# Sparse attention with a Swish layer: pair 1's first keys by the hardware queues, as f32

## Chip, cores and metric

One core of one Trainium2 chip. The kernel is launched once, and the metric is the device time of that launch in microseconds. Shorter is better.

## What is computed

Four batches of eight heads, 768 positions, 64 values per head, all inputs f32. Each position attends to its near neighbours (distance under 16) and to 24 block keys (the elementwise maximum over 32 keys) whose values are block means. The result goes through a two-matrix layer with a Swish of its own factor per channel.

```python
k_sum = k.reshape(B, H, nb, block, D).max(axis=3)        # block = 32, nb = 24
v_sum = v.reshape(B, H, nb, block, D).mean(axis=3)
scores_l = scale * q @ k.T ; mask_l = abs(i - j) < 16
scores_s = scale * q @ k_sum.T + log(block)
a = softmax([where(mask_l, scores_l, -1e9), scores_s])
x = a @ [v, v_sum]                                       # -> [3072, 512]
h = x @ w_in                                             # d_ff = 2048
out = (h / (1 + exp(-beta * h))) @ w_out
```

## The kernel before

The matrix products run on TensorE in bf16. Heads go in pairs, two heads of 64 on the 128 partitions; pair 0 is heads 0 and 1. The order of the work on each engine is the order in which the code is written: no scheduler moves it.

Batch 0 is done in two halves of 384 positions, so that the first half can enter the layer early. The part of the code that the change touches is the start of that first half. For each pair, `turn0(g)` turns the keys and queries with TensorE transposes (`pk`, `pq` in PSUM) and copies them to `kw` and `qt`. `scores0(g)` adds the mask and the scores into PSUM and takes the exponential on ScalarE. `max_k` makes the block keys on VectorE, `sum_v` the block means of v on TensorE (`vm_ps`). `pq` and `vm_ps` take turns in two PSUM buffers of the tag "t": what takes a buffer waits for the copy that empties it. `keep_warm(n)` issues n matmuls whose result nobody reads.

The code between two calls sets the order: `keep_warm`, `turn0(0)`, `turn0(1)`, `keep_warm(2)`, `scores0(0)`, `scores0(1)`, `turn0(2)`, `turn0(3)`, `scores_blk(0)`, `sum_v(0)`, `scores0(2)`, `scores0(3)`, `sum_v(1)` and so on, later `sum_v(3)` and the first products with `w_in`. The copies of the keys of pairs 0, 1 and 3 are ScalarE's, the copies of the queries of pairs 0, 1 and 2 and of the keys of pair 2 are VectorE's.

Loads are issued by three engines, each with its own queue. SP and ScalarE have hardware queues, whose transfers keep the type: pair 0's keys come as f32 into `k_f32` by SP and pair 0's queries into `q_f32` by ScalarE. VectorE casts the keys to bf16, ScalarE the queries. All other loads of batch 0 are issued by GpSimd, whose queue casts f32 to bf16 on the way (`load_k`, `load_q`, `load_v`), in the order of the code: keys of pair 1, queries of pair 1, keys of pairs 2 and 3, queries of pairs 2 and 3, v, `w_in`.

The cast also lays pair 0's keys out anew: in bf16 they stand as (j h d) instead of (h j d), so that one 128x128 transpose turns two heads at once. `turn` knows this as `packed`, six transposes a pair instead of twelve. The profile shows the tile `k_f32` as `k_f`, and `q_f32` as `q_f`.

Of the kernel before, what the change touches and what calls it, by code (L numbers as in the profile page):

```python
# [12 lines left out]
def kernel(  # L13
# [10 lines left out]
    nc = tc.nc  # L24
    ctx.enter_context(tc.manual_schedule(engines={getattr(mybir.EngineType, e) for e in ("SP", "Pool", "PE", "DVE", "Activation")}))
    P = 128
    f32 = mybir.dt.float32
# [4 lines left out]
    B, H, S, D = q.shape  # L32
    block = 32
    W = 16
# [6 lines left out]
    J = S // P  # L41
# [21 lines left out]
    const = ctx.enter_context(tc.tile_pool(name="consts", bufs=1))  # L63
# [9 lines left out]
    k_run = k.rearrange("b h (p j) d -> b p h (j d)", j=J)  # L73
    q_run = q[0].rearrange("h (u p j) d -> u p h (j d)", p=QP, j=JQ)
# [8 lines left out]
    kw_bufs = [const.tile([P, 2, NC, P], bf16, name=f"kw{i}") for i in range(NKW)]  # L83
    qt_bufs = [const.tile([P, nch, 2, QT], bf16, name=f"qt{i}") for i in range(NKW)]
    qk_bufs = {nm: const.tile([P, H, J * D], bf16, name=nm + "_all") for nm in "kq"}
    k_f32 = const.tile([P, 2, J * D], f32, name="k_f32")
    q_f32 = const.tile([QP, 2, JQ * D], f32, name="q_f32")
    q0_bufs = [const.tile([QP, H, JQ * D], bf16, name=f"q0_{i}") for i in range(2)]

    nat = {}  # L90
    dve, act, pool = nc.vector.tensor_copy, nc.scalar.copy, nc.gpsimd.tensor_copy
# [3 lines left out]
    def load_k(b, g, n=1):  # L95
        t = qk_bufs["k"][:, 2 * g:2 * (g + n)]
        nc.gpsimd.dma_start(out=t, in_=k_run[b, :, 2 * g:2 * (g + n)])
        for i in range(n):
            nat[("k", b, g + i)] = t[:, 2 * i:2 * i + 2]

    def load_q(u, g, n=1):
        t = q0_bufs[u][:, 2 * g:2 * (g + n)]
        nc.gpsimd.dma_start(out=t, in_=q_run[u, :, 2 * g:2 * (g + n)])
        for i in range(n):
            nat[("q", "q2")[u], 0, g + i] = t[:, 2 * i:2 * i + 2]
# [17 lines left out]

    beta_tmp = wpool.tile([k2, P], f32, name="beta_tmp")
    v_tail = wpool.tile([W, D], f32, name="v_tail")
    nc.sync.dma_start(out=k_f32[:], in_=k_run[0, :, 0:2])
    nc.scalar.dma_start(out=q_f32[:], in_=q_run[0, :, 0:2])
    nc.sync.dma_start(out=v_tail[:], in_=v_rows[0, H * S - W:H * S])
    nc.sync.dma_start(out=beta_tmp[:], in_=moe_beta.rearrange("(a p) -> a p", p=P))

# [20 lines left out]
    def fill(t, x):  # L151
        nc.vector.memset(t, x)

    def select(t, base, pattern, cm, op=ALU.is_ge, value=0.0):
        nc.gpsimd.affine_select(out=t, in_=t, compare_op=op, fill=value, base=base, pattern=pattern, channel_multiplier=cm)
# [2 lines left out]
    zero(identity)  # L158
    fill(near2, 1.0)
    fill(near, 1.0)  # L160
    load_k(0, 1)
    select(identity, 0, [[-1, P]], 1, ALU.not_equal, 1.0)
    load_q(0, 1)
    load_k(0, 2, 2)
    load_q(0, 2, 2)
    select(near2, -1, [[1, P + 32]], -1)
# [94 lines left out]
    def kw_of(b, g):  # L261
        return kw_bufs[(b * npair + g) % NKW]

    def flat_k(b, g):
        return kw_of(b, g)[:, 0].rearrange("p c f -> p (c f)")

    def flat_q(g):
        return qt_bufs[g].rearrange("p m r f -> p (m r f)")
# [18 lines left out]
    def psum(shape, dt, name, tag):  # L287
        if tag == "t":
            return ps.tile(shape, dt, name=name, tag="t", bufs=2)
        flat = take(name, dt)[:, 0, 0:math.prod(shape[1:])]  # L290
        if len(shape) == 2:
            return flat
        return flat.rearrange("p (a b) -> p a b", b=shape[2])

    def turn(nm, b, g, dst, copy, tag="t", packed=False):
        t = nat.pop((nm, b, g))
        n, js = t.shape[0], t.shape[2] // D
        p = psum([P, js, n], bf16, "p" + nm, tag)
        for j in range(js):
            if packed:  # L300
                nc.tensor.transpose(p[:, j], t.rearrange("p h f -> p (h f)")[:, j * P:(j + 1) * P], identity[0:n, 0:n])
                continue
            for h in range(2):
                nc.tensor.transpose(p[h * D:(h + 1) * D, j], t[:, h, j * D:(j + 1) * D], identity[0:n, 0:n])
        copy(out=dst.rearrange("p (t j) -> p t j", j=js), in_=p.rearrange("p j t -> p t j"))  # L305
# [98 lines left out]
    kq_of = {}  # L404

    def turn0(g, copy_k=act, copy_q=dve):
        turn("k", 0, g, flat_k(0, g)[:, W:W + S], copy_k, "big", g == 0)
        turn("q", 0, g, flat_q(g)[:, 0:HQ], copy_q, "t", g == 0)

    def scores0(g):  # L410
# [292 lines left out]
        for _ in range(n):  # L703
            nc.tensor.matmul(w_ps[:, 0:w], warm[:, 0:P], warm[:, 0:w], start=True, stop=True)

    for nm, t, copy, src in (("k", qk_bufs["k"][:, 0:2], dve, k_f32), ("q", q0_bufs[0][:, 0:2], act, q_f32)):
        nat[(nm, 0, 0)] = t
        copy(out=t.rearrange("p h f -> p (h f)").rearrange("p (j h d) -> p h j d", h=2, d=D),
             in_=src.rearrange("p h (j d) -> p h j d", d=D))
    keep_warm(9)  # L710
# [3 lines left out]
    fill(neg_m[0:W, 0:P], NEG)  # L714
    keep_warm(2)
    turn0(0)
    turn0(1)
    keep_warm(2)
    max_k(0, 0)
    scores0(0)  # L720
    max_k(0, 1)
    scores0(1)
    act(out=ve_bufs[0][0:W, HC, 0:D], in_=v_tail[:])
    turn0(2, dve, dve)
    turn0(3, act, act)
    scores_blk(0)
# [100 lines left out]
    for b in range(B):  # L827
# [6 lines left out]
        main, t = [], 0.0  # L834
# [33 lines left out]
        if b == 0:  # L868
# [23 lines left out]
            for g in pairs:  # L892
                t = dn0 + OT * TK[g] if g < 2 else up1 + TK[g]
# [15 lines left out]
        elif nxt < B:  # L909
            for g in pairs:  # L910
                t = (2.6, 6.5, 10.4, 14.3)[g]
# [60 lines left out]
```

## Time and profile before

| | |
|---|---|
| median of 3 runs | 213.62 us (213.19 to 213.9) |
| the profiled execution | 212.49 us |
| its span, from the first to the last instruction | 210.8 us |
| TensorE, matmuls | 201.4 us busy, 96% |
| VectorE | 109.4 us, 52% |
| ScalarE | 118.4 us, 56% |
| GpSimd | 80.9 us, 38% |
| granted TensorE clock | 1.000 |

Busy time counts an engine's instructions, without register, branch, semaphore and DMA-issuing ones on most engines. In the profile PE is TensorE's matmul, PEld its weight load, DVE VectorE, ACT ScalarE, POOL GpSimd and SP the engine that only issues transfers; a trailing q (ACTq) is the engine's issuing side. A row of the timeline gives start, duration, engine, line, operation, output<-input, shapes, the count merged into it (x6), and in brackets the idle time before it with what ended it. A row of the chain gives start, duration and what the end waited for.

### The profile page before, as it was taken

The numbers are of one execution on the slowest core, as the hardware profiler recorded it, in microseconds if no ns is written. First come the engines' busy times: TensorE is split into PE (matmuls) and PEld (weight loads), VectorE is DVE, ScalarE is ACT, GpSimd is POOL, SyncE is SP. The second block draws the span as 40 slices with busy tenths as digits, with TensorE's granted clock in tenths as the row PEclk, the third lists the DMA queues.
The fourth block names the chain that finished last, engine by engine and source line by source line (L and its number), as shares of the span: only waits on it lengthen the run. The fifth ranks groups of instructions, "written<-read, shape, count | busy, mean of one in ns | idle before, by whom it ended". The sixth has DMA issues, their size and how long they took to land.

```text
span 210.8 us, 4942 instructions
## 1 busy us (share of the span) xinstructions
PE 201.4 (96%) x2025; PEld 112.9 (54%) x2044; DVE 109.4 (52%) x311; ACT 118.4 (56%) x170; POOL 80.9 (38%) x116
## 2 busy tenths in 40 slices
PE   7798999999999999999999999999999999999993
PEld 2466654556545556565555456655555566654452
DVE  4877999997959869234726755514425000002120
ACT  3673988159797386668337256669165176640000
POOL 7995997495055399886300093000000000000000
PEclk9999999999999999999999999999999999999999
DMA  6999999999959999999994799900342500001212
GB/s 156 172 150 203 203 183 195 200 153 209 163 89 147 115 198 138 149 164 157 154 202 128 128 153 154 182 13 0 120 107 72 155 2 3 0 0 51 103 50 100
DMA packets 92055, 26.46 MB, mean 126 GB/s; under 512 B 81136, under 2 KB 89088, under 8 KB 92032
## 3 DMA queue, kind: packets, MB, share of 16 engines
q0 software_dynamic: 63888, 13.34, 77.5%
q1 hardware_dynamic: 27792, 12.40, 31.0%
q10 hardware_dynamic: 352, 0.39, 0.6%
q8 instruction: 16, 0.26, 0.5%
q14 instruction: 7, 0.06, 0.1%
HBM read 27.27 MB, written 6.29 MB: 159 GB/s over the span
## 4 chain that ended last, share of the span: by engine, by line
PE 90%; DMA 5%; issue 1%; DVE 1%; ACT 0%
PE h_ps L609 36%; PE o_ps L660 34%; PE o_ps L691 5%; PE h_ps L639 4%; DMA ve<-in_v_dram 3%; PE av_ps L566 3%; DMA k_f<-in_k_dram 2%; PE s_ps L521 2%; PE s_ps L504 1%; PE vm_ps L370 1%; PE px L487 1%; PE vm_ps L380 1%; PE av_ps L450 0%; PE s_ps L416 0%; DVE qt L305 0%
## 5 line engine op out<-in xcount | busy, mean ns | idle before, releaser
L609 PE MATMUL h_ps<-xT,w_in_sb 128*128 128x384 bf16 x464 | 76.7, 326 | 0.0
L660 PE MATMUL o_ps<-w_out_sb,h_sb 128*128 128x512 bf16 (+2 forms) x336 | 72.9, 369 | 1.8 <-issue 1.4
L621 ACT ACTIVATE h_sb<-h_ps,beta_sb 128x768 bf16<-128x768 f32 (+1 forms) x80 | 59.2, 773 | 23.3 <-PE h_ps L609 19.4
L609 PEld LDWEIGHTS <-w_in_sb 128*128 128x128 bf16 x464 | 45.0, 98 | 29.7
L660 PEld LDWEIGHTS <-h_sb 128*128 128x128 bf16 x352 | 32.6, 98 | 35.6
L679 DVE COPY o_sb<-o_ps 128x512 f32<-128x512 f32 x5 | 3.5, 691 | 38.6 <-PE o_ps L660 38.6
L547 DVE TENSOR_TENSOR attn<-attn,band 128x768 bf16<-128x768 bf16 x24 | 13.0, 556 | 19.0 <-ACT attn L496 17.3
L110 POOL DMA_DIRECT2D q_all<-in_q_dram x24 | 20.2, 869 | 3.5 <-DMA ve<-in_v_dram 3.1
L679 ACT COPY o_sb<-o_ps 128x512 f32<-128x512 f32 x15 | 8.9, 596 | 22.3 <-PE o_ps L660 17.1
L496 ACT ACTIVATE attn<-s_ps 128x768 bf16<-128x768 f32 x24 | 17.7, 814 | 3.3 <-PE s_ps L521 2.2
L116 POOL DMA_DIRECT2D ve<-in_v_dram x16 | 16.8, 1059 | 5.0 <-DMA w_out_sb<-in_moe_w_out_dram 3.9
L110 POOL DMA_DIRECT2D k_all<-in_k_dram x16 | 13.9, 885 | 2.1 <-DMA ve<-in_v_dram 1.7
L342 DVE TENSOR_TENSOR half<-kw 128x384 bf16<-128x384 bf16 x16 | 5.8, 364 | 15.0 <-DMA kw<-k_all 14.9
L363 DVE COPY vo<-ve 64x780 bf16<-64x780 bf16 (+3 forms) x30 | 11.4, 381 | 0.7
L576 DVE TENSOR_TENSOR x_nat<-av_ps,r 128x768 bf16<-128x768 f32 x12 | 11.5, 957 | 0.5
L691 PE MATMUL o_ps<-w_out_sb,h_sb 128*128 128x512 bf16 x45 | 11.1, 380 | 0.3 <-issue 0.2
L672 ACT COPY o_sb<-o_ps 128x384 f32<-128x384 f32 x1 | 0.5, 478 | 19.0 <-PE o_ps L660 19.0
L240 ACT ACT_TABLE_LOAD x7 | 9.0, 1283 | 0.1
L639 PE MATMUL h_ps<-xT,w_in_sb 128*128 128x384 bf16 x48 | 8.3, 326 | 0.0
L352 DVE COPY kw<-kw 128x192 bf16<-128x192 bf16 (+2 forms) x32 | 7.5, 281 | 0.0
L489 ACT COPY xT<-px 128x384 bf16<-128x384 bf16 (+1 forms) x5 | 3.0, 606 | 8.0 <-PE px L487 8.0
L566 PEld LDWEIGHTS <-attn 128*64 128x64 bf16 x288 | 5.2, 111 | 3.4 <-issue 2.1
(125 smaller groups left out, 193.8 us busy)
## 6 DMA issues: line engine op xcount, KB each, us to landing
out_dram<-o_sb SPq DMA_DIRECT2D x23, 256.0 KB, 2.8
ve<-in_v_dram POOLq DMA_DIRECT2D x12, 192.0 KB, 6.7
q_all<-in_q_dram POOLq DMA_DIRECT2D x24, 96.0 KB, 6.6
w_in_sb<-in_moe_w_in_dram POOLq DMA_DIRECT2D x8, 256.0 KB, 9.4
k_all<-in_k_dram POOLq DMA_DIRECT2D x16, 96.0 KB, 6.9
w_out_sb<-in_moe_w_out_dram POOLq DMA_DIRECT2D x4, 256.0 KB, 6.9
w_out_sb<-in_moe_w_out_dram POOLq DMA_DIRECT2D x2, 512.0 KB, 9.3
k_all<-in_k_dram POOLq DMA_DIRECT2D x5, 192.0 KB, 9.4
```

Source lines behind the costliest of these rows:

```text
L110: nc.gpsimd.dma_start(out=t[:, :, h], in_=(k_row if nm == "k" else q_row)[b, g, :, h])
L116: nc.gpsimd.dma_start(out=ve_bufs[b % 2][:, lo:hi, 0:D], in_=src)
L496: nc.scalar.activation(out=at[(b, g)][:, par].rearrange("p m h f -> p h m f"), in_=sv, func=ACTF.Exp, scale=scale)
L547: nc.vector.tensor_mul(out=a, in0=a, in1=band[:, par])
L566: nc.tensor.matmul(ov[par * QT:(par + 1) * QT, h, m], a[:, par, m, h], t[:, PC * g + nch * h + m0 + m], start=True, stop=True)
L576: nc.vector.tensor_mul(out=x.rearrange("p m h d -> p h m d"), in0=ov[:, :, :, 0:D], in1=r[:, :, :, None].to_broadcast([P, 2, n, D]))
L609: nc.tensor.matmul(big[:, j, 0:MG], w_in_sb[:, ki, ni * P:(ni + 1) * P], xT[b][:, ki, tok:tok + MG], start=(ki == 0), stop=(ki == k1 - 1))
L621: nc.scalar.activation(out=hb.rearrange("p (k m) -> p k m", m=MG), in_=big[:, j:j + w, 0:MG], func=ACTF.Silu, scale=beta_sb[:, ni:ni + 1])
L639: nc.tensor.matmul(h_open[(u, i)][:, j, 0:MG], w_in_sb[:, ki, i * P:(i + 1) * P], xT[b][:, ki, t0 + j * MG:t0 + (j + 1) * MG], start=start ...
L660: nc.tensor.matmul(o_ps[:, c0:c1], h_bufs[(u, ni * w // k2)][:, ni % (k2 // w), ms * P:(ms + 1) * P], w_out_sb[:, ni, c0:c1], start=(ni == ...
L679: (act if u + 1 < len(units) else dve)(out=o_sb[:], in_=o_ps[:])
L691: nc.tensor.matmul(o_ps, h_bufs[(u, ni * w // k2)][:, ni % (k2 // w), ms * P:(ms + 1) * P], w_out_sb[:, ni], start=(ni == 0), stop=(ni == ...
```

## The change

Pair 0's keys and queries come as two transfers each, one per head: head 1 by ScalarE's queue, head 0 by SP's. Pair 1's keys no longer come by GpSimd's queue: they come as f32 into a new tile `k1_f32`, one head per hardware queue, behind the others. ScalarE casts them to bf16 into the packed layout, after the cast of pair 0's queries. So pair 1's keys are turned with six transposes, too. In GpSimd's queue the load of pair 1's queries takes the place of the load that is gone, ahead of the `select` that makes the identity matrix.

```diff
-    k_f32 = const.tile([P, 2, J * D], f32, name="k_f32")
+    k_f32, k1_f32 = (const.tile([P, 2, J * D], f32, name=nm) for nm in ("k_f32", "k1_f32"))
...
-    nc.sync.dma_start(out=k_f32[:], in_=k_run[0, :, 0:2])
-    nc.scalar.dma_start(out=q_f32[:], in_=q_run[0, :, 0:2])
+    nc.scalar.dma_start(out=k_f32[:, 1:2], in_=k_run[0, :, 1:2])
+    nc.sync.dma_start(out=k_f32[:, 0:1], in_=k_run[0, :, 0:1])
+    nc.scalar.dma_start(out=q_f32[:, 1:2], in_=q_run[0, :, 1:2])
+    nc.sync.dma_start(out=q_f32[:, 0:1], in_=q_run[0, :, 0:1])
+    nc.scalar.dma_start(out=k1_f32[:, 1:2], in_=k_run[0, :, 3:4])
+    nc.sync.dma_start(out=k1_f32[:, 0:1], in_=k_run[0, :, 2:3])
     nc.sync.dma_start(out=v_tail[:], in_=v_rows[0, H * S - W:H * S])
...
-    load_k(0, 1)
+    load_q(0, 1)
     select(identity, 0, [[-1, P]], 1, ALU.not_equal, 1.0)
-    load_q(0, 1)
     load_k(0, 2, 2)
...
     def turn0(g, copy_k=act, copy_q=dve):
-        turn("k", 0, g, flat_k(0, g)[:, W:W + S], copy_k, "big", g == 0)
+        turn("k", 0, g, flat_k(0, g)[:, W:W + S], copy_k, "big", g < 2)
...
-    for nm, t, copy, src in (("k", qk_bufs["k"][:, 0:2], dve, k_f32), ("q", q0_bufs[0][:, 0:2], act, q_f32)):
-        nat[(nm, 0, 0)] = t
+    for nm, g, t, copy, src in (("k", 0, qk_bufs["k"][:, 0:2], dve, k_f32), ("q", 0, q0_bufs[0][:, 0:2], act, q_f32),
+                                ("k", 1, qk_bufs["k"][:, 2:4], act, k1_f32)):
+        nat[(nm, 0, g)] = t
```

ScalarE's order from the kernel's start, before. The rows show line, operation, output<-input and what the instruction waits for; DMAHW names the completion of a transfer of the hardware queues.

```order
L127 DMA q_f_93<-in_q_dram 96x2x256
L708 ACT_TABLE_LOAD
L708 CAST q_0_94<-q_f_93 96x2x4x64 [waits DMAHW0_49]
L305 COPY kw_82<-pk 128x768 [waits PE_49]
L305 COPY kw_83<-pk 128x768 [waits PE_49]
L422 ACTIVATE attn_237<-s_ps 128x960 [waits PE_49]
L422 ACTIVATE attn_253<-s_ps 128x960 [waits PE_49]
```

The same place now (`kw_82` and `kw_83` are the turned keys of pairs 0 and 1, `k_f_93` is the new f32 tile of pair 1):

```order
L126 DMA k_f_92<-in_k_dram 128x384
L128 DMA q_f_94<-in_q_dram 96x256
L130 DMA k_f_93<-in_k_dram 128x384
L712 ACT_TABLE_LOAD [waits DMAHW3_49]
L712 CAST q_0_95<-q_f_94 96x2x4x64 [waits DMAHW2_49]
L712 CAST k_all<-k_f_93 128x2x6x64 [waits DMAHW5_49,DMAHW4_49]
L308 COPY kw_82<-pk 128x768 [waits PE_49]
L308 COPY kw_83<-pk 128x768 [waits PE_49]
L425 ACTIVATE attn_236<-s_ps 128x960 [waits PE_49]
```

ScalarE issues three transfers instead of one, a cast stands between the query cast and the first key copy, and the table load, which waited for nothing, waits for one of the two halves of pair 0's queries; the query cast waits for the other.

GpSimd's order at the same place, before and then now:

```order
L97 DMA k_all<-in_k_dram 128x2x384
L155 ISA
L155 AFFINE_SELECT identity<-identity 128x128 [waits DVE_49]
L103 DMA q_0_94<-in_q_dram 96x2x256
L97 DMA k_all<-in_k_dram 128x4x384
L103 DMA q_0_94<-in_q_dram 96x4x256
```

```order
L103 DMA q_0_95<-in_q_dram 96x2x256
L159 ISA
L159 AFFINE_SELECT identity<-identity 128x128 [waits DVE_49]
L97 DMA k_all<-in_k_dram 128x4x384
L103 DMA q_0_95<-in_q_dram 96x4x256
```

One load is gone, and every later load of GpSimd's queue moves up by one place.

## Prediction

> **What bounds the kernel now.** I read the engines' shares first, then the chain that ended last in order of time, then the timeline of the first 20 us, where the change lies, and last the load of the DMA engines there.
>
> ```profile
> PE 201.4 (96%) x2025; PEld 112.9 (54%) x2044; DVE 109.4 (52%) x311; ACT 118.4 (56%) x170; POOL 80.9 (38%) x116
> ```
>
> TensorE is the bound. It can only be made shorter where it waits, and nearly all its waiting is at the start. The chain there (start, us, what):
>
> ```profile
> 0.82 4.19 DMA k_f<-in_k_dram
> ...
> 5.86 6.26 DMA ve<-in_v_dram
> 12.11 0.04 issue
> 12.15 0.38 PE vm_ps L380 x13
> ...
> 17.07 0.64 issue
> ...
> 18.17 0.33 PE vm_ps L380 x14
> ```
>
> Pair 0's keys (`k_f`) start TensorE's real work, but the end hangs on something later: the first piece of v, issued at 5.86, lands at 12.11, and `sum_v(0)` on TensorE starts at 12.15. From there to 17.07 the chain is TensorE without a break. So the question is what the change does to the moment 12.15. The instructions that lead to it:
>
> ```profile
> 1.27 3.94 PE L704 MATMUL w_ps<-warm 128*128 128x512 bf16 x11 [1.27 <-DVE warm L149]
> 1.28 1.28 ACT L708 ACT_TABLE_LOAD   x1 [1.28 <-PEq L956]
> 1.32 0.86 POOL L97 DMA_DIRECT2D k_all<-in_k_dram  x1 [0.79 <-POOLq L956]
> 4.54 0.62 ACT L708 CAST q<-q_f 96x512 bf16<-96x512 f32 x1 [1.98 <-DMA q_f<-in_q_dram]
> 5.04 0.72 DVE L708 CAST k_all<-k_f 128x768 bf16<-128x768 f32 x1 [1.32 <-DMA k_f<-in_k_dram]
> 5.81 0.51 PE L301 MATMUL pk<-identity,k_all 128*128 128x128 bf16 x6 [0.60 <-DVE k_all L708]
> 6.16 0.34 PE L301 MATMUL pq<-identity,q 96*128 96x96 bf16 x4
> 6.36 1.50 ACT L305 COPY kw<-pk 128x768 bf16<-128x768 bf16 x2 [1.20 <-PE pk L301]
> 6.42 0.53 PE L304 MATMUL pk<-identity,k_all 128*64 128x128 bf16 x12
> 6.88 0.36 PE L304 MATMUL pq<-identity,q 96*64 96x96 bf16 x8
> 7.17 0.61 PE L704 MATMUL w_ps<-warm 128*128 128x512 bf16 x2
> 8.11 0.38 PE L420 MATMUL s_ps<-qt,kw 64*128 64x128 bf16 x8
> 8.43 0.58 PE L416 MATMUL s_ps<-neg_m,identity 128*128 128x480 bf16 x2
> 8.94 0.38 PE L420 MATMUL s_ps<-qt,kw 64*128 64x128 bf16 x8
> 9.37 0.36 PEld L304 LDWEIGHTS <-k_all 128*64 128x64 bf16 x12 [0.20 <-DMA k_all<-in_k_dram]
> 9.94 0.96 DVE L305 COPY kw<-pk 128x768 bf16<-128x768 bf16 x1 [0.40 <-PE pk L304]
> 10.65 0.36 PE L304 MATMUL pq<-identity,q 96*64 96x96 bf16 x8 [0.75 <-DMA q<-in_q_dram]
> 11.05 0.56 DVE L305 COPY qt<-pq 128x384 bf16<-128x384 bf16 x1
> 11.38 0.80 ACT L305 COPY kw<-pk 128x768 bf16<-128x768 bf16 x1 [0.90 <-PE pk L304]
> ```
>
> The reader is to see three things. Pair 1's keys (the 12 transposes at 6.42) cost no wait today. From 9.37 on TensorE follows landings: keys of pairs 2 and 3, queries at 10.65, v. And the table load on ScalarE runs at 1.28, while it would wait for queries anyway.
>
> **The change part by part.** *The loads.* 384 KB of f32 leave GpSimd's queue, which cast them on the way, and come by the hardware queues. The rates (stretch, busy times, granted clock, DMA share, GB/s):
>
> ```profile
> 1.00:2.00 1.00, 0.73 (x2) 0.28 (x3) 1.00 (x14) 0.72 (x1) 0.68 (x1) 1.00 0.12 16
> 2.00:3.00 1.00, 1.00 (x4) 0.35 (x3) 0.63 (x7) 0.56 (x1) 0.91 (x3) 1.00 0.75 192
> 3.00:4.00 1.00, 1.00 (x4) 0.41 (x3) 0.51 (x5) 0.00 (x0) 1.00 (x3) 1.00 1.06 361
> 5.00:6.00 1.00, 0.40 (x5) 0.20 (x5) 0.96 (x4) 0.16 (x1) 0.97 (x3) 1.00 1.31 164
> 7.00:8.00 1.00, 1.00 (x12) 0.41 (x10) 0.80 (x3) 0.85 (x2) 1.00 (x2) 1.00 1.32 194
> ```
> ```profile
> k_f<-in_k_dram SPq DMA_DIRECT2D x1, 384.0 KB, 4.2
> k_all<-in_k_dram POOLq DMA_DIRECT2D x1, 192.0 KB, 5.0
> ```
>
> A pair's keys count 384 KB where they land as f32 and 192 KB where they land as bf16, so the GB/s of casting loads stand for twice as many read. At 3 to 4 us the hardware queues move 361 GB/s; at 5 to 8 us GpSimd's moves 164 to 194, which is 328 to 388 read. Pair 1's 393 kB thus take 1.09 us by the one way and 1.01 to 1.20 by the other: the engines, busy without a gap from 3 us, have the same work ahead of v, within 0.1 us. Term 0; v still lands near 12.1. GpSimd also issues all later loads 0.86 us earlier (the row at 1.32). I cost that at nothing: v's first piece spends 6.26 us between issue and landing, in the queue. If that cover were gone, it would be a gain of at most 0.86.
>
> *Pair 0's keys by both queues at once.* They land before 5.01; at best the 6 transposes start when the warm-up matmuls end (1.27+3.94 = 5.21) instead of 5.81. Worth nothing by itself: the next steps wait for ScalarE.
>
> *ScalarE, the part that decides.* In the changed order the cast of pair 0's queries has two halves to wait for, and one of these two waits stands on the table load ahead of it. The load, done by 2.56 today, now begins only when that half has landed. Behind it, in order on ScalarE: query cast, the new cast of pair 1's keys, then the two `kw` copies. When do the halves land? Not before 4.5, when the lone query load did (its cast follows at 4.54). By bytes, the same 384 KB of keys and 192 KB of queries go first as before `k_f` landed at 5.01, and I add 0.1 for a third load that the other queue may already be serving: 4.5 to 5.1. I take 4.9, nearer the end that rests on bytes. Then 1.28 for the table, 0.62 for the queries, and 0.80 for 128x768 keys (bounds 0.72, VectorE's row for the same shape, and 0.93, ScalarE's 0.62 scaled by 768/512), with 0.05 between them: the key cast ends at T = 4.9+2.75 = 7.65 (7.2 to 8.0). Pair 1's keys themselves land about 6.1 (5.01 plus 1.09), before ScalarE is ready for them at 6.85, so their landing is hidden.
>
> *What hangs on T.* TensorE idles from pair 0's key transposes to the query cast, and again to T. Then: 0.05 to start, 0.35 for 6 transposes (5.81 to 6.16; the packed form replaces 12 that took 0.46, a gain of 0.11), 0.29 for the queries (6.88 to 7.17), and 2.09 from the warm-up pair through both `scores0` (7.17 to 8.94, and 0.32 as from 8.11 to 8.43). Pair 2's keys start at T+2.78. VectorE's `kw` copy follows 0.57 later (9.37 to 9.94), takes 0.96, and the `qt` copy 0.56: done at T+4.87. `sum_v(0)` writes the PSUM buffer that this copy empties, so it starts no earlier than T+4.87 = 12.52. Before, the same copy ended at 11.05+0.56 = 11.61, under the cover of v's landing at 12.11; that cover is now used up, and 0.37 us sticks out (T from 7.2 to 8.0: 12.1 to 12.9, so 0 to 0.7). ScalarE's two exponentials move back by about 1 us, into its 0.90 us of idle time before pair 3's copy at 11.38.
>
> *Sum:* loads 0, earlier issue 0, packing inside T, ScalarE +0.37. The profiled execution took 212.49 us (span 210.8), 1.13 below the median of 213.62; on the median's scale 213.99, so 214.0. One unknown can swallow it: the 0.64 us at 17.07 for which the profile names no releaser. A gap tied to a moment would absorb the shift, one tied to TensorE's place would not. I let it pass on.
>
> **The rivals.** *Slower: GpSimd's queue holds up pair 1's keys.* Hardware and software queues use the same engines, and the software queue's first packets come between 3.5 and 4.0 (half-microsecond stretches from 3.5 and from 4.0; packets, MB, share):
>
> ```profile
> q1 hardware_dynamic: 128, 0.15, 84.2%
> q0 software_dynamic: 18, 0.01, 19.4%
> ```
> ```profile
> q0 software_dynamic: 81, 0.06, 99.6%
> q1 hardware_dynamic: 56, 0.04, 28.3%
> ```
>
> Until now the hardware queues were nearly done by then. After the change 983 kB go there (384+192+384 KB), of which 569 are moved by 4.0 (16+192+361); 414 are left. At 361 GB/s alone this is 1.15 us, and landing follows about 0.9 later, as for `k_f`: 6.1. With two thirds of the engines 6.6, still hidden behind 6.85. With half, 7.2: T = 8.05, `sum_v(0)` at 12.92, +0.77, 214.4. With a third, 8.3: T = 9.15, 14.02, +1.87, 215.5. It decides from a landing of 7.1 on. For it: 81 packets against 56 in the second stretch. Against: the hardware's 56 were its last ones. By the Trainium skill (DMA: Bandwidth & Descriptors, section "Queues, rings and completion order") each engine serves its queues in turn and drains a whole packet, typically 9 to 17 descriptors, before it switches. By that rule the software queue could take two thirds, and the sum would be +1.87 instead of +0.37; no row here shows both kinds full for long. The same end is reached if the query half lands after 5.2.
>
> *Faster: the software queue was a limit of its own.* Then v lands 1.1 us earlier, and the queries of pairs 2 and 3 too. T must also be early, and is not: with halves at 4.5, T = 7.25 gives 12.12. Only if the table load does not hold ScalarE either does T fall to 6.95 (landing 6.1 plus 0.85), `sum_v(0)` to 11.8: -0.35, 213.3; with the 0.64 gap gone as well 212.6. Against: the read rates, equal within 10%.
>
> *The shift is swallowed at 17.07:* 213.6. For it, the gap has no cause in the rows; against, that nothing says it is tied to a moment.
>
> **How the numbers follow.** 0.3% is 0.64 us, about what a measurement of this kernel can tell from no change. Small shift, 213.6 to 214.3: 0.46. Swallowed: 0.12. Slower by shared queues or late halves, 214.4 to 215.5: 0.32. Faster, 212.4 to 213.3: 0.10. A tenth of the first case ends beyond 0.64 us by its own bounds, and part of the fast case stays inside. So faster 0.08, same 0.56, slower 0.36. The range runs from 213.2 (just under the nearer end of the fast case) to 215.2 (most of the way from half to a third); about 0.08 is left out below and 0.08 above.
>
> **What would show it.** Right: the table load starts near 4.9, not 1.28; the first `kw` copy near 7.7 instead of 6.36; TensorE idle before the first queries and before pair 1's keys; the wait before `sum_v(0)` no longer ends on v but on the `qt` copy, near 12.5; all of v lands as before. Wrong: a table load that still runs by 2.6; v landing a microsecond earlier; pair 1's key cast starting after 7.1 with ScalarE idle before it, which is the slower rival.

## The result, and the profile after

The changed kernel takes 213.95 us (median of 22 executions, 212.5 to 215.77). The kernel before takes 212.88 us (22 executions, 211.42 to 214.89). The ratio is 1.0056, with a 95% interval of 1.0036 to 1.0076: slower by about 1.2 us. The forecast was 214.0 us, that is +0.37 us on a median of 213.62. The absolute number fits by luck: the median of before came out 0.74 us lower with more executions, and the shift was about three times the forecast.

The profiled execution of the changed kernel took 213.09 us, span 211.4 us. The engines' busy times, in the order that they had before:

```profile
PE 204.5 (97%) x2038; PEld 113.5 (54%) x2038; DVE 109.3 (52%) x311; ACT 119.1 (56%) x171; POOL 79.8 (38%) x115
```

TensorE is still the bound. The chain that ended last begins elsewhere (start, us, what): not on v, but on the f32 keys of pair 1, issued at 1.76 and landed 5.59 us later.

```profile
1.76 5.59 DMA k_f<-in_k_dram
...
7.43 0.84 ACT k_all L712
8.27 0.05 issue
8.32 0.51 PE pk L304 x6
```

The timeline around it, for the engines that wait:

```profile
4.98 1.28 ACT L712 ACT_TABLE_LOAD   x1 [4.98 <-DMA q_f<-in_q_dram]
5.94 0.85 PE L304 MATMUL pk<-identity,k_all 128*128 128x128 bf16 x6
6.27 0.62 ACT L712 CAST q<-q_f 96x512 bf16<-96x512 f32 x1
7.43 0.83 ACT L712 CAST k_all<-k_f 128x768 bf16<-128x768 f32 x1 [0.54 <-DMA k_f<-in_k_dram]
8.17 1.49 ACT L308 COPY kw<-pk 128x768 bf16<-128x768 bf16 x2
8.32 0.51 PE L304 MATMUL pk<-identity,k_all 128*128 128x128 bf16 x6 [0.92 <-ACT k_all L712]
13.18 0.39 PE L383 MATMUL vm_ps<-ve,A_avg 128*32 128x64 bf16 x14 [0.53 <-DVE qt L308]
```

The reader is to see that the table load waits until 4.98 as forecast, but that ScalarE then stands idle once more, 0.54 us, for pair 1's keys. The first `kw` copy at 8.17 and `sum_v(0)` (the row of `vm_ps`) at 13.18 follow from the late key cast. In the kernel before, `sum_v(0)` went on at 12.15.

Why do the keys land at 7.35? The packets of the queues show it. These are two half-microsecond stretches, from 4.0 and from 4.5, of the changed kernel (packets, MB, share; q1 is SP's queue, q10 ScalarE's, q0 GpSimd's):

```profile
q0 software_dynamic: 47, 0.02, 43.3%
q1 hardware_dynamic: 32, 0.04, 32.3%
q10 hardware_dynamic: 29, 0.04, 29.3%
...
q0 software_dynamic: 41, 0.02, 38.9%
q10 hardware_dynamic: 36, 0.06, 31.9%
q1 hardware_dynamic: 30, 0.05, 29.3%
```

The two hardware queues together move 61 and 66 packets, 0.08 to 0.11 MB, in half a microsecond. The 361 GB/s that they had nearly alone in the kernel before would be 0.18 MB. The software queue has 41 to 47 packets beside them. So once GpSimd's queue runs, the hardware queues keep about half of what they had: the slower rival's "with half, 7.2".

One thing is in no trace of the changed kernel, only in the list of its executions, which gives a mean granted TensorE clock for each:

| kernel | executions at 0.992 or less | their mean, us | mean of the others, us |
|---|---|---|---|
| changed | 13 of 22 | 214.45 | 213.16 |
| before, in four later comparisons | 2 of 96 | | |

The means leave out the one execution of each kernel that was slow, over 1.5% above its kernel's fastest; over the other 21 they are 212.76 before and 213.89 after. At full clock the changed kernel is thus 213.16 - 212.76 = 0.40 us slower (the 9 executions leave some 0.2 us of uncertainty), and the 12 left with a lower clock add 12/21 x 1.28 = 0.73 us. By this estimate, most of the loss is not the later start itself, but a clock that falls in more than half of the executions. The profiled execution is one at full clock and doesn't show it. (The clocks of the 22 executions of before are not listed; the 96 come from the comparisons below.)

### The profile page after: what moved, and what is told of

It is laid out like the page before. It is cut to its first block, busy times and chain, and to the rows that moved or that the text cites. A ratio compares the mean times of both kernels' runs of the same rounds, so it can differ in the third digit from the quotient of the medians.

```text
span 211.4 us, 4960 instructions
## 1 busy us (share of the span) xinstructions
PE 204.5 (97%) x2038; PEld 113.5 (54%) x2038; DVE 109.3 (52%) x311; ACT 119.1 (56%) x171; POOL 79.8 (38%) x115
## 4 chain that ended last, share of the span: by engine, by line
PE 88%; DMA 7%; DVE 1%; ACT 1%; issue 1%; SPq 0%; ACTq 0%
PE h_ps L612 36%; PE o_ps L663 32%; PE o_ps L694 5%; DMA xT<-x_nat 5%; PE h_ps L642 3%; DMA k_f<-in_k_dram 3%; PE av_ps L569 2%; PE s_ps L524 2%; PE s_ps L419 1%; PE vm_ps L373 1%; PE px L490 1%; PE pk L307 1%; PE s_ps L423 1%; PE vm_ps L383 1%; PE s_ps L507 1%
## 5 line engine op out<-in xcount | busy, mean ns | idle before, releaser
L663 PE MATMUL o_ps<-w_out_sb,h_sb 128*128 128x512 bf16 (+2 forms) x352 | 75.8, 370 | 0.0
L694 PE MATMUL o_ps<-w_out_sb,h_sb 128*128 128x512 bf16 x48 | 11.6, 380 | 0.0
L402 DVE COPY vo<-vm 32x780 bf16<-32x780 bf16 x12 | 7.3, 607 | 0.2
```

The lines of the kernel that those rows point to most:

```text
L663: nc.tensor.matmul(o_ps[:, c0:c1], h_bufs[(u, ni * w // k2)][:, ni % (k2 // w), ms * P:(ms + 1) * P], w_out_sb[:, ni, c0:c1], start=(ni == ...
L694: nc.tensor.matmul(o_ps, h_bufs[(u, ni * w // k2)][:, ni % (k2 // w), ms * P:(ms + 1) * P], w_out_sb[:, ni], start=(ni == 0), stop=(ni == ...
```

## The experiments

Diffs are against the changed kernel unless another is named. Ratios are against the kernel before on the same chip.

**Without the table load's wait.** A one-column ScalarE copy ahead of the casts takes the table load off the query half.

```diff
+    act(out=turnstile[:], in_=warm[:, 0:1])
     for nm, g, t, copy, src in (("k", 0, ...
```

> The changed kernel with a one-column copy on ScalarE ahead of the casts, so that the table load waits for no query half. If the table load is what made the change slower, the key copies move up: pair 1's key cast then ends about 0.8 us earlier, sum_v(0) starts near 12.4 instead of 13.18, and the time falls by 0.3 to 0.8 us, most of the way back to the kernel before. If the landing of pair 1's keys (7.35 us in the changed kernel, where 6.1 was predicted) is what binds, the key cast still starts at about 7.4, sum_v(0) stays at 13.1 to 13.2, and the ratio stays near 1.005.

Measured: 214.38 us, ratio 1.0088 (1.0054 to 1.0122), no gain, as the second of the two theories had it. The query cast runs 1.4 us earlier, and the time goes into the next wait (timeline):

```profile
4.87 0.62 ACT L713 CAST q<-q_f 96x512 bf16<-96x512 f32 x1 [1.16 <-DMA q_f<-in_q_dram]
7.71 0.83 ACT L713 CAST k_all<-k_f 128x768 bf16<-128x768 f32 x1 [2.23 <-DMA k_f<-in_k_dram]
13.46 0.39 PE L383 MATMUL vm_ps<-ve,A_avg 128*32 128x64 bf16 x14 [0.53 <-DVE qt L308]
```

What binds is the landing of pair 1's keys. 7 of its 10 executions have the lower clock.

**The split alone.** The kernel before, with pair 0's two loads by halves; pair 1's keys stay in GpSimd's queue.

```diff
-    nc.sync.dma_start(out=k_f32[:], in_=k_run[0, :, 0:2])
-    nc.scalar.dma_start(out=q_f32[:], in_=q_run[0, :, 0:2])
+    nc.scalar.dma_start(out=k_f32[:, 1:2], in_=k_run[0, :, 1:2])
+    nc.sync.dma_start(out=k_f32[:, 0:1], in_=k_run[0, :, 0:1])
+    nc.scalar.dma_start(out=q_f32[:, 1:2], in_=q_run[0, :, 1:2])
+    nc.sync.dma_start(out=q_f32[:, 0:1], in_=q_run[0, :, 0:1])
```

> The kernel before with the first part of the change alone: pair 0's keys and queries by head on two hardware queues, pair 1's keys by GpSimd's queue as before. The table load waits for a query half here too (about 4.9, query cast done by 6.9). Theory of the table load: TensorE's transposes of pair 1 start near 7.2 instead of 6.42, and the time is half or more of the change's loss, ratio 1.002 to 1.005. Theory of the landing: pair 1's keys are there by 6.3, the late query cast uses up slack (qt copy done by 12.2, v lands at 12.1), and the ratio is 0.998 to 1.002.

Measured: 212.13 us, ratio 0.9977 (0.9946 to 1.0008), and no execution of 12 at the lower clock. The table load waits here too, and it costs nothing:

```profile
4.83 1.28 ACT L710 ACT_TABLE_LOAD   x1 [4.83 <-DMA q_f<-in_q_dram]
6.12 0.62 ACT L710 CAST q<-q_f 96x512 bf16<-96x512 f32 x1
...
12.71 0.38 PE L382 MATMUL vm_ps<-ve,A_avg 128*32 128x64 bf16 x13 [0.49 <-DMA ve<-in_v_dram]
```

`sum_v(0)` still ends its wait on v. So neither the split nor the table load is what costs.

**Pair 1's keys alone.** The kernel before, with pair 1's keys as f32 behind pair 0's undivided loads, run in two comparisons.

```diff
     nc.scalar.dma_start(out=q_f32[:], in_=q_run[0, :, 0:2])
+    nc.scalar.dma_start(out=k1_f32[:, 1:2], in_=k_run[0, :, 3:4])
+    nc.sync.dma_start(out=k1_f32[:, 0:1], in_=k_run[0, :, 2:3])
...
-    load_k(0, 1)
+    load_q(0, 1)
     select(identity, 0, [[-1, P]], 1, ALU.not_equal, 1.0)
-    load_q(0, 1)
```

> The kernel before with the second part of the change alone: pair 0's loads whole as before (keys by SP, queries by ScalarE's queue), pair 1's keys as f32 by head behind them. The query cast waits for one transfer, so the table load runs early. Theory of the landing: pair 1's keys land near 7.3, their cast on ScalarE ends near 8.2, sum_v(0) starts near 13.1, ratio 1.003 to 1.007 as for the whole change. Theory of the table load: its wait is gone, so the ratio is 0.998 to 1.002.

Measured: 212.9 us, ratio 1.0015 (0.9986 to 1.0044); the expected landing at 7.3 did not come. The stretches from 4.0, 4.5 and 5.0 say why:

```profile
q10 hardware_dynamic: 73, 0.11, 61.8%
q1 hardware_dynamic: 59, 0.08, 45.6%
...
q1 hardware_dynamic: 85, 0.12, 65.0%
q10 hardware_dynamic: 46, 0.05, 30.5%
q0 software_dynamic: 16, 0.01, 13.8%
...
q0 software_dynamic: 125, 0.06, 91.8%
q1 hardware_dynamic: 66, 0.05, 36.9%
```

GpSimd issued its first load at 1.38, as in the changed kernel, but the software queue's first packets come only at 4.8 instead of 3.7. Until then the hardware queues have the engines to themselves, and the key cast starts at 6.39. The second comparison was to tell whether that late start belongs to the order of loads or to one execution.

> The same kernel as the one with pair 0's whole loads and pair 1's keys behind them, run once more. It tells whether the late start of the software queue there (4.79 us) belongs to that order of loads or to that execution. If to the execution, the profile may show a start near 3.7, then pair 1's keys land near 7.3, sum_v(0) is at 13.0 or later, and the ratio, which is over other executions, stays between 0.999 and 1.005. If it belongs to the order of loads, the start is after 4.5 again, the keys land by 6.6, sum_v(0) is at 12.0 to 12.5, ratio 0.998 to 1.003.

Measured: 213.06 us, ratio 1.002 (0.9992 to 1.0048). The software queue starts after 4.5 again, and the cast at 6.71, 1 of 12 executions at the lower clock. `sum_v(0)` was expected at 12.0 to 12.5, but waits for v in this profile and goes on only at 13.23, as late as in the changed kernel. So both profiles of this order start late, while all five profiles that keep the changed kernel's order of loads and its issue at 1.38 start before 4.0 (both of the changed kernel, and those without the table load's wait, with pair 0 first and with matmuls in the waits). The late start goes with the order of the hardware loads, in two profiles against five; by what means was not found.

**Pair 0 first.** Pair 1's keys are cast by VectorE behind `scores0(0)`, and `turn0(1)` comes behind it, so that pair 0's work no longer waits for them; with the early table load.

```diff
+    act(out=turnstile[:], in_=warm[:, 0:1])
...
-                                ("k", 1, qk_bufs["k"][:, 2:4], act, k1_f32)):
+                                ("k", 1, qk_bufs["k"][:, 2:4], dve, k1_f32)):
         nat[(nm, 0, g)] = t
+        if g == 1:
+            continue
...
     turn0(0)
+    keep_warm(2)
+    scores0(0)
+    max_k(0, 0)
+    dve(out=qk_bufs["k"][:, 2:4]..., in_=k1_f32...)
     turn0(1)
-    keep_warm(2)
-    max_k(0, 0)
-    scores0(0)
```

> The changed kernel with the loads as they are, but nothing of pair 0 behind pair 1's keys: table load early, pair 1's keys cast by VectorE, and scores0(0) with its exponential ahead of turn0(1). If the loss is only the in-order wait for late keys, pair 0's exponential starts near 7.2, pair 1's transposes near 8.2, sum_v(0) waits for v again near 12.1 to 12.3, and the ratio to the kernel before is 0.995 to 1.001. If the loss comes from elsewhere (v landing later, TensorE's clock), the ratio stays at 1.004 or more.

Measured: 213.3 us, ratio 1.0037 (1.0009 to 1.0066), none of 12 at the lower clock. TensorE still waits for the keys, 1.02 us, but later, and `sum_v(0)` comes at 12.72:

```profile
8.90 0.51 PE L304 MATMUL pk<-identity,k_all 128*128 128x128 bf16 x6 [1.02 <-DVE k_all L727]
12.72 0.39 PE L383 MATMUL vm_ps<-ve,A_avg 128*32 128x64 bf16 x14 [0.56 <-DVE qt L308]
```

The order of the work hides some of the late landing at the start, not all. The expected ratio of 0.995 to 1.001 did not come: with no execution at the lower clock this kernel is no faster than the changed one's executions at full clock.

**GpSimd's queue later, by one step and by two.** The first load of GpSimd's queue is issued behind two of its `select`s (at 2.26 instead of 1.38), or behind all of them (at 3.02). Everything else is the changed kernel. If the hardware queues lose their time to the software queue, they must get it back.

```diff
-    load_q(0, 1)
     select(identity, 0, [[-1, P]], 1, ALU.not_equal, 1.0)
-    load_k(0, 2, 2)
-    load_q(0, 2, 2)
     select(near2, -1, [[1, P + 32]], -1)
     select(near2, 31, [[-1, P + 32]], 1)
+    load_q(0, 1)
+    load_k(0, 2, 2)
+    load_q(0, 2, 2)
```

(one step; in two steps the three loads stand behind the `select`s of `A_avg` as well)

> The changed kernel with two of the selects (identity and near2) ahead of GpSimd's first load, so that it is issued at about 2.3 us instead of 1.4; a middle dose between the changed kernel and the one with the first load at 3.0. If the two kinds of queues share the engines evenly, the software queue's first packets come about 4.3 to 4.6 instead of 3.7, pair 1's keys land about 6.7 to 7.0 (7.35 in the changed kernel, 6.6 or less with the load at 3.0), and their cast no longer waits or waits under 0.2 us; the keys of pairs 2 and 3 land about 0.6 later, near 11.3, and cost TensorE up to 0.9 us of wait there: sum_v(0) 13.0 to 14.0, ratio 1.003 to 1.008. If the keys' landing had nothing to do with the software queue's start, they land at 7.3 to 7.9 again and sum_v(0) comes at 13.2 or later with the keys of pairs 2 and 3 on time.

Measured, one step: 212.84 us, ratio 1.0011 (0.9986 to 1.0036), none of 12 at the lower clock. The software queue has 3 packets from 4.5 to 5.0 (first rows) and 126 in the half microsecond after it, and the key cast waits for nothing:

```profile
q1 hardware_dynamic: 83, 0.12, 65.0%
q10 hardware_dynamic: 47, 0.06, 34.1%
q0 software_dynamic: 3, 0.00, 2.2%
```
```profile
4.78 1.28 ACT L712 ACT_TABLE_LOAD   x1 [4.78 <-DMA q_f<-in_q_dram]
6.60 0.83 ACT L712 CAST k_all<-k_f 128x768 bf16<-128x768 f32 x1
7.49 0.51 PE L304 MATMUL pk<-identity,k_all 128*128 128x128 bf16 x6 [0.39 <-ACT k_all L712]
12.35 0.39 PE L383 MATMUL vm_ps<-ve,A_avg 128*32 128x64 bf16 x14 [0.53 <-DVE qt L308]
```

This is the case that the prediction took as the likeliest: table load near 4.9, hidden landing, T = 7.43, `sum_v(0)` at 12.35. With 0.9 us on one queue's first issue, no loss is left that these executions can tell from none. (The intervals of this kernel and of the changed one touch only at 1.0036.) The expected cost of 0.3 to 0.8% for late keys of pairs 2 and 3 did not come: TensorE turns them at 10.30 without a wait.

> The changed kernel with GpSimd's mask selects ahead of its first load, so that its queue's transfers begin about 1.8 us later, when the hardware queues are nearly through. Theory of shared engines: with no software packets beside them, pair 1's keys land by 6.5 instead of 7.35; their cast then starts when ScalarE is free, at about 6.9 (the table load still waits for a query half), ends near 7.7, sum_v(0) starts near 12.6, and the ratio falls to 1.001 to 1.004. Theory that the hardware queues are slow by themselves (three transfers each): the landing stays at 7.2 to 7.5 and the ratio at 1.005 or, with later software loads, above.

Measured, two steps: 215.38 us, ratio 1.0108 (1.0062 to 1.0155), not the expected 1.001 to 1.004. The keys are cast at 6.58 without a wait, as shared engines would have it, but the next loads of the delayed queue, the keys and queries of pairs 2 and 3, are now late:

```profile
12.00 0.53 PE L307 MATMUL pk<-identity,k_all 128*64 128x128 bf16 x12 [1.64 <-DMA k_all<-in_k_dram]
13.35 0.53 PE L307 MATMUL pq<-identity,q 96*64 96x96 bf16 x8 [0.82 <-DMA q<-in_q_dram]
```

And this trace caught a fall of the clock. The rows are stretches of 3.4 us (busy times of TensorE, its weight load, VectorE, ScalarE, GpSimd; granted clock, DMA share, GB/s):

```profile
6.50:9.90 3.40, 2.90 (x35) 1.42 (x32) 2.11 (x5) 2.63 (x5) 3.40 (x5) 1.00 1.10 136
9.90:13.30 3.40, 0.98 (x21) 0.60 (x20) 1.37 (x3) 1.61 (x3) 1.50 (x3) 0.98 2.03 142
13.30:16.70 3.40, 3.35 (x52) 2.03 (x54) 2.40 (x8) 1.57 (x3) 2.26 (x4) 0.51 2.87 156
16.70:20.10 3.40, 3.40 (x92) 2.46 (x92) 1.44 (x5) 2.40 (x4) 1.95 (x3) 1.00 1.34 201
```

After 3.4 us in which TensorE was busy for 0.98, the clock is halved for the next 3.4 us, in which TensorE has work all the time. One such fall is 0.5 x 3.4 / 214 = 0.008 of the mean clock from 1, the 0.992 that the changed kernel's executions show. The Trainium skill (TensorE: Matmul & The Clock Gate, "Part 1: The HAM clock gate") says that a free-running window of about 3.4 us decides, and that the clock halves after at least one idle window. The length of the fall agrees with that. The idle part does not, if the stretch before the fall is such a window: it was 29% busy, and the longest wait in it was 1.64 us. Of its 21 matmuls 12 are transposes; whether those count as work for the clock was not tested.

**The two together.** All `select`s first, and the early table load.

> As the run before, and the table load freed by a one-column copy on ScalarE at the start. If late keys and table load together are the whole loss, the key cast ends near 7.1, sum_v(0) waits for v again near 12.1 to 12.4, and the ratio is 0.998 to 1.002. If something else makes the change slower, it stays at 1.004 or more.

Measured: 215.05 us, ratio 1.0114 (1.0069 to 1.0159), 4 of 6 executions at the lower clock. The key cast ends at 7.49, but late keys of pair 1 and the table load are not the whole loss here. `sum_v(0)` is earlier than with the late queue alone (14.08 for 15.21), since its waits for the keys and queries of pairs 2 and 3 are 1.00 and 0.72. The clock falls here too, after a window that was about half busy:

```profile
9.90:13.30 3.40, 1.68 (x46) 1.23 (x46) 1.89 (x4) 1.69 (x3) 1.98 (x4) 0.99 2.65 152
13.30:16.70 3.40, 3.40 (x42) 1.44 (x36) 2.50 (x7) 2.03 (x4) 2.48 (x4) 0.51 3.06 154
```

**Both kernels once more**, each with another profile.

> The kernel before, unchanged, timed against itself: the ratio should be 1.000 with an interval of some 0.3% either way, and its profile tells whether the 0.64 us stall of TensorE at 17.07 is there in every execution. If it is there again, the changed kernel, whose profile lacks it, gains it back; if it is absent, TensorE's first product with w_in starts near 19.4 instead of 20.08, and the change's full cost of about 1 us shows in the times.

> The changed kernel again, one profile: does the landing of pair 1's keys at 7.35 repeat? Theory of shared engines: software packets from about 3.7 on, landing between 7.0 and 7.8, sum_v(0) near 13.2. If it lands by 6.5 here, the first profile was an accident of that execution.

The kernel before gave 212.7 us, ratio 0.9992 (0.9965 to 1.0018), the changed one 213.3 in one execution, at full clock. Its key cast starts at 7.97, and `sum_v(0)` at 13.72, so the late landing repeats. The first `w_in` product starts at 21.13. The second profile of before starts its first `w_in` product at 19.04, 1.04 us earlier than the first (20.08), and has the same span, 210.9 us. The lead is given back to later landings:

```profile
42.02 0.98 PE L320 MATMUL pk<-identity,k_all 128*64 128x128 bf16 x24 [0.20 <-DMA k_all<-in_k_dram]
58.45 0.57 PE L504 MATMUL s_ps<-qt,kw 64*128 64x64 bf16 x24 [0.49 <-DMA qt<-q_all]
```

**Is an earlier start worth anything?** The split alone, with the early table load.

```diff
+    act(out=turnstile[:], in_=warm[:, 0:1])
     for nm, t, copy, src in (("k", qk_bufs["k"][:, 0:2], dve, k_f32), ...
```

> The kernel before with pair 0's loads by halves (the split alone, which measured 0.9977 [0.9946, 1.0008]) and a one-column ScalarE copy that takes the table load away from the wait for a query half. If a lead at the start is lost to later landings, as the second profile of the kernel before showed (start 1.04 us earlier, same span), the table load near 2.2 and pair 1's transposes earlier bring nothing: ratio 0.995 to 1.001, span 210.4 to 210.9. If the start were the bound, sum_v(0) would come 0.3 to 0.8 us earlier than the 12.71 of the split alone, and the time would fall by as much: ratio 0.993 to 0.996.

Measured: 212.86 us, ratio 1.0022 (0.9994 to 1.005). `sum_v(0)` goes on at 11.61 where the split alone had 12.71, the first `w_in` product starts at 18.73, and the span is 211.1 us. The lead is gone by 60 us:

```profile
11.61 0.38 PE L382 MATMUL vm_ps<-ve,A_avg 128*32 128x64 bf16 x13 [0.18 <-DMA ve<-in_v_dram]
...
58.86 0.53 PE L506 MATMUL s_ps<-qt,kw 64*128 64x64 bf16 x24 [0.86 <-DMA qt<-q_all]
```

3 of its 12 executions have the lower clock, which is not explained: in its profile TensorE waits little before 13 us.

**The waits filled with matmuls.** The loads and ScalarE's work stay as in the changed kernel; TensorE gets five matmuls more that nobody reads, for the time in which it waits for pair 1's keys. If its idleness lets the clock fall, this must make the falls rare without bringing the keys any earlier.

```diff
-    keep_warm(9)
+    keep_warm(11)
...
     turn0(0)
+    keep_warm(3)
     turn0(1)
```

> The changed kernel with five more matmuls that nobody reads, two behind the warm-up and three between pair 0's and pair 1's transposes, where TensorE waits 0.9 to 1.7 us for pair 1's keys. They change neither the loads nor what ScalarE does. The changed kernel shows a mean granted clock of 0.992 or less in 13 of its 22 executions, which take 1.3 to 2.7 us more than those at 1.000; the kernel before shows it in hardly any. If the clock falls because TensorE stands idle for pair 1's keys, these executions become rare (at most 2 in 12) and the ratio falls from 1.0056 to 1.001 to 1.004, what the later start alone costs (pair 1's transposes at 8.3 or later, sum_v(0) at 13.2 or later, span 211.2 to 211.8, as in the profiled execution at 1.000). If the fall of the clock has another cause, about half of the executions keep it and the ratio stays between 1.004 and 1.009.

Measured: 212.93 us, ratio 1.0028 (1.0001 to 1.0054), 1 of 12 executions at the lower clock instead of 13 of 22. The keys landed even later than in the changed kernel's profile, and `sum_v(0)` started later:

```profile
6.66 0.81 PE L707 MATMUL w_ps<-warm 128*128 128x512 bf16 x3
7.85 0.83 ACT L712 CAST k_all<-k_f 128x768 bf16<-128x768 f32 x1 [1.43 <-DMA k_f<-in_k_dram]
8.74 0.51 PE L304 MATMUL pk<-identity,k_all 128*128 128x128 bf16 x6 [1.26 <-ACT k_all L712]
13.60 0.39 PE L383 MATMUL vm_ps<-ve,A_avg 128*32 128x64 bf16 x14 [0.53 <-DVE qt L308]
```

By the ratios half of the loss goes with the clock, while the start is as late as ever. The two intervals overlap (1.0036 to 1.0076, and 1.0001 to 1.0054), so the count of executions is the stronger sign. The changed kernel was not timed in this comparison, which ran on another chip than the other experiments; a share of the chip in the count is not excluded. What is left, 0.28% or 0.6 us (0.0 to 1.1), fits the 0.40 us of the changed kernel's executions at full clock. (The changed kernel's executions at the lower clock took 0.6 to 2.5 us more than its mean at full clock, not the 1.3 to 2.7 that the expectation gives.) No version measured here is clearly faster than the kernel before.

## Why the prediction was right or wrong

The chance that it gave the measured case, slower by over 0.3%, was 0.36; it took a shift of +0.37 us as likelier. That 213.95 stands beside 214.0 is luck: the two causes of the loss, the late landing and the clock, are not in its sum.

- *Table load behind a query half: right, and worth nothing.* Start forecast 4.9, measured 4.98 and, in the second profile, 4.83. But with the wait removed the time did not fall, and in the split alone it cost nothing.
- *Pair 1's keys land at 6.1, hidden: wrong.* This is the step that failed. Measured 7.35, and the casts in other profiles start at 7.71, 7.85 and 7.97. The prediction had the cause as its slower rival, with the half share at 7.2 and the point of decision at 7.1, and gave it 0.32. The error lay in taking 361 GB/s, measured while the software queue was nearly silent (its 18 packets from 3.5 on were its first), for a time when it runs. The row with 81 packets against 56 already stood for the rival and was set aside because the 56 were the hardware's last.
- *From T to `sum_v(0)`, T+4.87: right.* Key cast done at 8.27, `sum_v(0)` at 13.18: 4.91. With the later queue 7.43 and 12.35: 4.92. The wait moved from v to the `qt` copy, as forecast.
- *Earlier issue of GpSimd's loads, cost 0: wrong in kind.* It was costed as at best a gain. The same issue 0.9 us later, behind two `select`s, left a loss of 0.11% (-0.14 to 0.36), since the early load is what contends.
- *A shift passes on to the end: half right.* The start is 1.03 us later in the profile (`sum_v(0)` at 13.18 for 12.15), and at full clock the time is only 0.40 us longer on average. In the first profile the first `w_in` product was just 0.24 us later (20.32 for 20.08), because the 0.64 us at 17.07, which was to pass the shift on or swallow it, is absent. In the second profile a delay does pass on: that product is 1.05 us later (21.13), and a product with `w_out` still 1.08 later (66.11 for 65.03). A lead does not pass on: two profiles show it lost to the landings of later batches.
- *The granted clock: missing.* No step asked whether a longer wait of TensorE would cost clock. It is the larger part of the loss, about 0.73 of 1.13 us by the executions' own clocks, and with the waits filled it is nearly gone (1 of 12 executions). In which stretch the clock falls in the changed kernel is not shown; only the traces of the two kernels with the late queue caught a fall.
- *v as before: right, as far as two pairs of profiles show.* The first piece was under cover. GpSimd's last load of `w_in`, which waits for the last piece of v, went on at 16.92 instead of 18.25, and that looks like the sign that the prediction took for its faster rival. But in the second profiles it went on at 17.46 in the changed kernel and at 17.33 in the kernel before, so the lead of 1.3 us belongs to the execution.

The rule of the Trainium skill that the prediction weighed (DMA: Bandwidth & Descriptors, "Queues, rings and completion order") has each engine switch between its queues packet by packet. The traces agree that both kinds are served in turn; 47 packets beside 61 are nearer to an even share than to the two thirds that the prediction allowed the software queue, for which it shows no working. That a packet of these rows is a packet of that rule is not shown; the hardware's hold some 1 to 2 KB each.

## What to carry to other kernels

Before moving a load to an idle queue, look at which other queue wakes up while it is under way, and price the transfer by the shared rate from there on, not by the rate that the queue had alone. A small step in the other queue's first issue may then be worth more than the move itself, and too large a step makes its own loads late. When waits at the start grow, look at each execution's granted clock and not at one profile: here, with waits of 1 to 2 us, over half of the executions had a lower clock, and with five matmuls that nobody reads 1 of 12 had it.

## What was not expected of the hardware

- The granted clock halves for 3.4 us after a stretch in which TensorE was 29% busy (0.98 of 3.40), and also after one with 49% (1.68 of 3.40). Without the transposes, 12 of 21 matmuls and 36 of 46, the two stretches hold 0.45 and 0.53 us of work. Yet the second profile of the changed kernel has hardly any work between 5.64 and 8.86 but one group of 0.34 us, and its clock stayed at 1.000. What decides it in one execution is open.
- The software queue's first packets come 2.3 us after the issue in the changed kernel (1.38 to 3.7) and 3.4 us after the same issue behind other hardware loads (1.38 to 4.8). Issued at 2.26 and at 3.02 they come between 4.5 and 5.0, and issued at 3.02 with the early table load, after 5.0.
- A wait of TensorE that the profile gives as "issue" comes and goes between executions near the same place of the program: 0.64 us at 17.07 in the first profile of before and none in the second, 0.75 at 18.68 with pair 0 first, 0.86 at 19.42 with the waits filled, none in the first profile of the changed kernel and 0.21 at 19.16 in its second. Its cause stays open.
